# A fused attention and feed-forward kernel: other places for output steps, maxima and scales in a batch's first pair, none kept back in its last

## The chip, the cores and the metric

The kernel runs on one core of a Trainium2 chip. The metric is the device time of one execution in microseconds (us), the median of several runs; lower is better. The engines named here are TensorE (PE in the profile, its weight loads PEld), VectorE (DVE), ScalarE (ACT), GpSimd (POOL) and SyncE (SP), whose queue issues the DMAs.

## The reference

Sigmoid attention over 8 batches of 12 heads, 448 tokens and 64 columns, then a feed-forward layer with an ELU between two matrices (768 x 2048 and 2048 x 768). Everything is float32 at the borders.

```python
S = q.shape[2]
scores = np.matmul(q, k.transpose(0, 1, 3, 2)) / np.sqrt(q.shape[-1]) - np.log(S)
attn = 1.0 / (1.0 + np.exp(-scores))
x = np.matmul(attn, v)                     # (B, H, S, D), then to (B*S, H*D)
h = x @ w_in
g = np.where(h > 0.0, h, np.exp(np.minimum(h, 0.0)) - 1.0)
out = g @ w_out
```

## The kernel before

To keep float32 accuracy at the speed of float16 matmuls, nearly every operand is split into a high and a low float16 part (`split`: ScalarE writes the high part, VectorE the rest), and each product is made of three matmuls (high by high, and the two mixed ones). A split needs a scale, a power of two from the largest absolute value of the operand.

The twelve heads of a batch are worked on as six **pairs** (hp = 0 to 5). The batch loop over b = 1 to 7 does two things at once: the attention of batch b, and the second feed-forward matmul (`moe2`) of batch b-1, whose work is cut into **steps** of three matmuls of 128 x 384. Sixteen steps make one output tile; the sixteenth also issues the tile's eviction on VectorE (o, L537) and its output DMA. There are 96 steps where b is odd and 128 where it is even (`left`, L689). `fill(n)` puts n of them in. When the six pairs are through, the first feed-forward matmul of batch b (`moe1`, 288 matmuls on L499) follows.

TensorE, ScalarE, VectorE and SyncE take their instructions in the order in which the loop from L697 writes them (`tc.manual_schedule`, L685); each engine works through its own list in that order. GpSimd, and what is issued ahead of L685, is placed by the framework's scheduler. That concerns batch 1, whose first pairs still share the engines with the preparation of `w_out` (`load_w_out`, lines so, wo, L138 to L157, and splits on L121/L122).

For one pair n the order of the loop before is:

- `scores(0)`, `soften(0)`, `scores(1)`, `soften(1)`: six matmuls each into psc (two buffers of PSUM), then a sigmoid on ScalarE (sg, L395), the high part on ScalarE (at, L413) and the low part on VectorE (at, L414).
- `third()`: for pair n+1 the splits of q and k (nat) and of v (vn), and the DMA transpose of nat on SP. It needs the scales of pair n+1. The loads of pair n+3 follow on SP.
- `fill(gap)`, the first gap: 8 steps in a batch's first pair, 5 in the others.
- `prepare_pair(n+2)`, here called the **maxima**: VectorE's reductions of rv and raw for pair n+2 (mx and mt, L125, then L307 and L310) and three diagonal tiles (dg, L105). It returns `second`.
- `scores(2)`, `soften(2)`, `scores(3)`, `soften(3)`; number 3 has half the rows and needs no split. `scores(3)` needs the psc buffer that the second sigmoid reads.
- in the last pair the first part of `rescale` (rr L448, xh L450).
- `fill(share - gap - tail)`.
- `second()`, here called the **product**: one TensorE matmul of the diagonal tiles (pb, L110), VectorE's reduction and four to five tiny operations (al to L285), and GpSimd's scalar operations (L319, L322, L324, L289) that make the scales for the next `third`. It returns `third`.
- `values(0..3)`: 18 matmuls (L433) and two in float32 (L425) into pav; `finish`: the split of pav into xh (ACT L121, DVE L122) and a maximum over it.
- in the last pair four steps that were kept back (`tail`), then `moe1`, which starts with `xh` of pair 0 and reaches that of pair 5 with its sixteenth matmul; after its eighteenth stands one pb matmul for the scale of the whole of xh.

PSUM: psc 2 x 2 banks, pav one bank, and the tag pm with three banks, shared by the output tiles, pb and most of moe1.

Of the kernel before, what the change touches and what calls it, by code (L numbers as in the profile page):

```python
# [32 lines left out]
def attention_ffn(  # L33
# [13 lines left out]
    NP = H // 2  # L47
# [208 lines left out]
    def load_qk(b, hp):  # L256

        h0 = 2 * hp
        raw = sb.tile([P, 2 * NC + 1, 2, D], F32, tag="raw", name=f"raw{b}_{hp}", bufs=2)
        for i, src in enumerate((q, k)):  # L260
            for j in range(2):
                nc.sync.dma_start(  # L262
                    raw[:, i * (NC + 1) :][:, :NC, j],
                    src[b, h0 + j, :SM].rearrange("(p c) d -> p c d", c=NC),
                )
            nc.sync.dma_start(
                raw[rows[i], NC], src[b, h0 : h0 + 2, SM:].rearrange("h r d -> r h d")
            )
        return raw

    def load_v(b, hp):
        rv = rvs[(b * NP + hp) % len(rvs)]
        main = rv[:, : 2 * NC].rearrange("p t d -> p (t d)")
        load_keys(main, [rv[r, 2 * NC + j] for j, r in enumerate(rows)], v, b, 2 * hp)
        return rv
# [270 lines left out]
    def out_scale(b, xs, xp, i=slice(0, NH)):  # L546
        if b % 2 == 0 and i.start == 0:
            oscs[0] = sb.tile([P, 3, NH], F32, tag="osc", name=f"osc{b}", bufs=2)
        j = b % 2
        o = oscs[0][:, j, i]  # L550
        nc.gpsimd.tensor_scalar(
            o, wop[:, i], wm[:, 0:1], 2.0 ** (10 - XTOP + 2 - GTOP - WTOP),
            op0=ALU.mult, op1=ALU.mult,
        )
        nc.gpsimd.tensor_scalar(o, o, xs[:, 0, NP - 1 :], xp, op0=ALU.mult, op1=ALU.mult)
        nc.gpsimd.tensor_copy(oscs[0][rows[j], 2, i], o[rows[j]])

    def moe2(b, g, wo):
        j = b % 2
        osc = oscs[0]  # L560

        def tokens(b, c):
            if c < NC:
                return out[b * S : b * S + SM].rearrange("(p c) m -> c p m", c=NC)[c]
            return out[b * S + SM : (b + 1) * S]

        def tile_of(c, i):
            if c < NC:
                return moe2_tile(
                    wo, [(slice(0, P), tokens(b, c))],  # L570
                    lambda gj, f: g[:, gj, f, c * P : (c + 1) * P],
                    osc[:, j, i : i + 1], i, f"{b}_{c}_{i}",
                )
            return moe2_tile(
                wo, [(rows[a], tokens(b - 1 + a, NC)) for a in range(2)],
                lambda gj, f: g[:, gj, f, SM:],
                osc[:, 2, i : i + 1], i, f"{b}_r_{i}",
            )

        for i in range(NH):  # L580
            for c in range(NC + j):
                yield from tile_of(c, i)
# [3 lines left out]
    def step(n):  # L586
        for _ in range(n):
            next(steps, None)
# [7 lines left out]
    def prepare_pair(n):  # L596

        if n >= len(pairs):
            return lambda: lambda: None
        b, hp = pairs[n]  # L600
        if hp == 0:
            xh_of[b] = sb.tile([P, NK, 2, S], F16, tag="xh", name=f"xh{b}", bufs=2)
            xs_of[b] = sb.tile([P, 3, NP], F32, tag="xs", name=f"xs{b}", bufs=2)
        scales = prepare(b, hp, *loaded.pop(n), xs_of[b])

        def second():
            transposed = scales()

            def third():
                ready[n] = transposed()  # L610

            return third

        return second
# [12 lines left out]
    def pair_of(n):  # L627
        b, hp = pairs[n]
        return Pair(b, hp, *ready.pop(n), xh_of[b], xs_of[b])

    def hidden(b, beside=None):

        xh, xs = xh_of.pop(b), xs_of.pop(b)
        whole = rescale(b, xh, xs)
        next(whole)
        yield
        xp, xr, rest = next(whole)
        m = sb.tile([P, 2, NF], F32, tag="msc", name=f"msc{b}")

        def first():  # L640
            rest()
            moe_scales(m, xs, xr)

        moe1(b, g, xh, m, first, beside)
        yield b, xs, xp
# [29 lines left out]
    third = prepare_pair(EXACT * NP + 1)()  # L675
# [9 lines left out]
    with tc.manual_schedule(engines={E.PE, E.Activation, E.DVE, E.SP}):  # L685
        for b in range(EXACT, B):
            out_scale(*of_moe2, slice(0, 1 if b == EXACT else NH))
            tiles = moe2(b - 1, g, wo)
            left = NF * NH * (NC + (b - 1) % 2)  # L689

            def fill(n):
                nonlocal left
                left -= n
                for _ in range(n):
                    next(tiles, None)

            for hp in range(NP):  # L697
                n = b * NP + hp
                share = left // (NP - hp)
                tail = 4 if hp == NP - 1 else 0  # L700
                p = pair_of(n)
                for t in range(2):
                    p.scores(t)
                    p.soften(t)
                third()
                if n + 3 < len(pairs):
                    loaded[n + 3] = load_qk(*pairs[n + 3]), load_v(*pairs[n + 3])

                gap = 8 if hp == 0 else 5
                fill(gap)  # L710
                second = prepare_pair(n + 2)
                for t in range(2, NC + 1):
                    p.scores(t)
                    p.soften(t)
                if b == EXACT and hp < NC:

                    step(3 if hp < NC - 1 else NF)
                if hp == NP - 1:
                    h = hidden(b)
                    next(h)  # L720
                fill(share - gap - tail)
                third = second()
                for t in range(NC + 1):
                    p.values(t)
                p.finish()
                fill(tail)
                if b == EXACT and hp == NC - 1:
                    out_scale(*of_moe2, slice(1, NH))
            of_moe2 = next(h)
        out_scale(*of_moe2)  # L730
        for _ in moe2(B - 1, g, wo):
            pass
# [30 lines left out]
```

## Time and profile before

| | |
|---|---|
| median of 3 runs | 1271.4 us (1270.87 to 1273.9) |
| profiled execution, its own time | 1270.86 us |
| its span, first to last instruction | 1269.1 us |
| mean granted TensorE clock | 0.984 |
| VectorE busy | 823.4 us, 65% of the span |
| ScalarE busy | 671.8 us, 53% |
| TensorE on moe1 (L499) / moe2 (L529, po) | 442.0 / 392.9 us |

All times within the execution are counted from the first instruction. A row of the timeline reads: start, duration, engine, line, operation, output<-inputs, shapes, number of merged instructions, and in brackets the idle time of the engine before it with what ended it. Matmuls overlap in the pipeline, so a row's duration reaches a little into the next row's start; distances are read from start to start. A row of the waits reads: engine, what waited, what it waited for, us in total, times, the longest. A row of the windows gives, for a stretch, its length, the busy time of each engine with the number of instructions, the granted TensorE clock, and the DMA share with GB/s.

### The profile page before, as it was taken

To read this page: it belongs to the slowest core of one execution; us is meant where nothing else is said; L and a number is where in the kernel's file an instruction comes from. 1 tells how busy PE (TensorE), PEld (TensorE's weight loads), DVE (VectorE), ACT (ScalarE), POOL (GpSimd) and SP (SyncE) were. 2 spreads that over 40 slices of the span, in tenths; PEclk is the share of its full clock that TensorE was granted. 3 is DMA by queue.
4 is the path that set the end of the run, shared out by engine and by line. 5 is a ranking of instruction groups with operands and counts; after the bars stand their busy time and mean duration, and the time that the engine had idled before them with its cause. 6 is when DMAs were issued, how large, how long until landed. Compare 5 with 4: busy or idle time off the path is not lost.

```text
span 1269.1 us, 19337 instructions
## 1 busy us (share of the span) xinstructions
PE 1200.2 (95%) x7246; PEld 610.5 (48%) x7246; DVE 823.4 (65%) x1872; ACT 671.8 (53%) x1015; POOL 84.1 (7%) x319
## 2 busy tenths in 40 slices
PE   5979868999999999999999999999999999999998
PEld 2324334445555554545455554545455554455565
DVE  5898989765766557775666646885576656765500
ACT  5867777643655337744555436654565435663400
POOL 0011001100000000010000000010000100100000
PEclk9889979999999999999999999999999999999999
DMA  8937423420233103340144201440034401410000
GB/s 229 281 100 222 126 77 80 100 49 1 60 84 89 37 1 83 89 86 1 37 92 92 50 1 43 105 103 7 1 86 92 92 1 22 106 43 7 1 25 26
DMA packets 213407, 89.76 MB, mean 71 GB/s; under 512 B 177472, under 2 KB 209216, under 8 KB 213312
## 3 DMA queue, kind: packets, MB, share of 16 engines
q1 hardware_dynamic: 213312, 88.51, 28.7%
q8 instruction: 57, 0.93, 0.3%
q14 instruction: 38, 0.31, 0.1%
HBM read 58.20 MB, written 11.01 MB: 55 GB/s over the span
## 4 chain that ended last, share of the span: by engine, by line
PE 78%; ACT 8%; DVE 7%; DMA 3%; issue 2%; SPq 2%; DVEq 0%; POOL 0%; ACTq 0%; POOLq 0%
PE ph L499 31%; PE po L529 25%; PE psc L384 7%; PE pav L433 6%; PE po_r L529 5%; PE pav L425 3%; ACT sg L395 2%; DMA stage<-in_moe_w_in_dram 2%; ACT at L413 1%; SPq L262 1%; PE pb L110 1%; ACT L395 1%; ACT e L511 1%; DVE e L514 1%; DMA so<-in_moe_w_out_dram 1%
## 5 line engine op out<-in xcount | busy, mean ns | idle before, releaser
L499 PE MATMUL ph<-xh,wi 128*128 128x448 f16 x2304 | 442.0, 353 | 6.1 <-DVE xh L122 2.4
L529 PE MATMUL po<-wo,g 128*128 128x384 f16 x2304 | 392.9, 328 | 0.0
L529 PEld LDWEIGHTS <-g 128*128 128x128 f16 x2688 | 257.2, 98 | 198.4 <-issue 36.3
L499 PEld LDWEIGHTS <-wi 128*128 128x128 f16 x2304 | 225.3, 98 | 218.4 <-issue 7.6
L511 ACT ACTIVATE e<-ph,msc 128x448 f32<-128x448 f32 x128 | 80.8, 633 | 211.7 <-PE ph L499 211.6
L414 DVE SCALAR_TENSOR_TENSOR at<-sg,at 128x896 f16<-128x896 f32 x126 | 137.2, 1090 | 84.5 <-ACT at L413 84.5
L395 ACT ACTIVATE sg<-psc,bias,sc 128x896 f32<-128x896 f32 (+1 forms) x168 | 166.6, 992 | 1.7
L513 DVE TENSOR_SCALAR e<-e 128x448 f32<-128x448 f32 x128 | 50.3, 394 | 170.8 <-ACT e L511 170.7
L121 ACT ACTIVATE xh<-pav,sc 128x448 f16<-128x448 f32 x48 | 30.3, 632 | 216.7 <-PE pav L425 216.7
L384 PE MATMUL psc<-qk 64*128 64x448 f16 x1008 | 116.6, 355 | 11.4 <-ACT sg L395 11.4
L413 ACT ACTIVATE at<-sg 128x896 f16<-128x896 f32 x126 | 119.8, 951 | 4.1
L121 ACT ACTIVATE g<-e,msc 128x384 f16<-128x384 f32 (+1 forms) x192 | 96.0, 534 | 6.0 <-DVE e L514 4.3
L122 DVE SCALAR_TENSOR_TENSOR g<-e,msc,g 128x384 f16<-128x384 f32 (+1 forms) x192 | 94.6, 521 | 0.6
L514 DVE SCALAR_TENSOR_TENSOR e<-ph,msc,e 128x448 f32<-128x448 f32 x128 | 87.3, 683 | 4.0
L384 PEld LDWEIGHTS <-qk 64*128 64x128 f16 x1008 | 41.7, 97 | 89.7 <-issue 60.2
L433 PE MATMUL pav<-at,vn 128*64 128x448 f16 x756 | 80.2, 357 | 0.0
L324 POOL TENSOR_SCALAR sc<-pw 128x1 f32<-128x1 f32 x42 | 12.4, 295 | 843.5 <-DVE pw L114 790.9
L529 PE MATMUL po_r<-wo,g 128*128 128x384 f16 x384 | 64.7, 326 | 0.0
L122 DVE SCALAR_TENSOR_TENSOR xh<-pav,sc,xh 128x448 f16<-128x448 f32 x48 | 32.7, 680 | 48.7 <-ACT xh L121 48.7
L433 PEld LDWEIGHTS <-vn 128*64 128x64 f16 x756 | 39.4, 110 | 50.0 <-issue 27.8
L122 DVE SCALAR_TENSOR_TENSOR nat<-raw,sc,nat 128x384 f16<-128x384 f32 (+1 forms) x126 | 59.1, 524 | 0.0
L121 ACT ACTIVATE nat<-raw,sc 128x384 f16<-128x384 f32 (+1 forms) x126 | 58.8, 529 | 0.0
(103 smaller groups left out, 852.7 us busy)
## 6 DMA issues: line engine op xcount, KB each, us to landing
stage<-in_moe_w_in_dram SPq DMA_DIRECT2D x16, 768.0 KB, 6.6
raw<-in_q_dram SPq DMA_DIRECT2D x96, 96.0 KB, 3.1
raw<-in_k_dram SPq DMA_DIRECT2D x96, 96.0 KB, 2.6
rv<-in_v_dram SPq DMA_DIRECT2D x48, 192.0 KB, 2.7
out_dram<-o SPq DMA_DIRECT2D x48, 192.0 KB, 2.1
wo<-in_moe_w_out_dram SPq DMA_DIRECT2D x19, 384.0 KB, 4.1
so<-in_moe_w_out_dram SPq DMA_DIRECT2D x13, 384.0 KB, 4.3
raw<-in_q_dram SPq DMA_DIRECT2D x48, 32.0 KB, 2.4
```

Source lines behind the costliest of these rows:

```text
L121: nc.scalar.mul(hi, src, s)
L122: nc.vector.scalar_tensor_tensor(lo, src, s, hi, op0=ALU.mult, op1=ALU.subtract)
L384: nc.tensor.matmul(psc[:, j, :S] if g < NC else psc[rows[j], 0, :S], kk[rows[j], o], qq[rows[j], :S], start=(n == 0), stop=(n == len(parts ...
L395: a = nc.scalar.activation(sg[:, :nb], psc[:, :nb, :S], AF.Sigmoid, bias=bias, scale=self.s_scale)
L413: nc.scalar.mul(hi, sg, 2.0**ATOP)
L414: nc.vector.scalar_tensor_tensor(lo, sg, 2.0**ATOP, hi, op0=ALU.mult, op1=ALU.subtract)
L433: nc.tensor.matmul(pav[rows[j], :S], vv[i][:, j * NC + g], sg[k][:, j], start=(g == 0 and n == 0), stop=False,)
L499: nc.tensor.matmul(ph[:, :S], wi[:, wj, c, f * P : (f + 1) * P], xh[:, c, xj], start=(n == 0), stop=(n == 3 * NK - 1),)
L511: a = nc.scalar.activation(e, ph[:, :S], AF.Exp, scale=inv)
L513: nc.vector.tensor_scalar(e, e, 1.0, -1.0, op0=ALU.min, op1=ALU.add)
L514: nc.vector.scalar_tensor_tensor(e, ph[:, :S], inv, e, op0=ALU.mult, op1=ALU.max)
L529: nc.tensor.matmul(po[:, :HM], lh(gj, f), wo[:, i, f, wj], start=(n == 0), stop=(n == 3 * NF - 1),)
```

## The change

In a batch's first pair (hp = 0) the first gap has 11 steps, and the pair 3 more in all; the other pairs share what is left. There the maxima come behind `scores`/`soften` 2 and 3, so behind VectorE's third split, and the product isn't issued at the pair's end but in the second pair, behind its first two `scores`; `third` follows it there after `soften` 0 and 1 as before. In every pair the two `scores` are written ahead of both `soften`, which leaves each engine's own order as it was. In the last pair no steps are kept back: all stand ahead of the product.

```diff
             for hp in range(NP):
                 n = b * NP + hp
-                share = left // (NP - hp)
-                tail = 4 if hp == NP - 1 else 0
+                share = left // (NP - hp) + (3 if hp == 0 else 0)
                 p = pair_of(n)
                 for t in range(2):
                     p.scores(t)
+                if hp == 1:
+                    third = second()
+                for t in range(2):
                     p.soften(t)
                 third()
                 if n + 3 < len(pairs):
                     loaded[n + 3] = load_qk(*pairs[n + 3]), load_v(*pairs[n + 3])
 
-                gap = 8 if hp == 0 else 5
+                gap = 11 if hp == 0 else 5
                 fill(gap)
-                second = prepare_pair(n + 2)
+
+                if hp:
+                    second = prepare_pair(n + 2)
                 for t in range(2, NC + 1):
                     p.scores(t)
                     p.soften(t)
+                if not hp:
+                    second = prepare_pair(n + 2)
...
-                fill(share - gap - tail)
-                third = second()
+                fill(share - gap)
+                if hp:
+                    third = second()
                 for t in range(NC + 1):
                     p.values(t)
                 p.finish()
-                fill(tail)
```

The steps of the six pairs, worked out from the code: where b is odd 16 each before, and 19, 15, 15, 15, 16, 16 now; where b is even 21, 21, 21, 21, 22, 22 before (the last with 4 kept back), and 24, 20, 21, 21, 21, 21 now.

## The prediction

> **What bounds the kernel now.** I read the page's first part, then TensorE's own waits, then the timeline wherever one of those waits stands.
>
> ```profile
> PE 1200.2 (95%) x7246; PEld 610.5 (48%) x7246; DVE 823.4 (65%) x1872; ACT 671.8 (53%) x1015; POOL 84.1 (7%) x319
> ...
> PE psc L384 <- ACT sg L395: 14.4, 13, 2.5
> PE pb L110 <- DVE dg L105: 11.6, 6, 2.0
> ```
>
> TensorE is busy for 95% of the span, so only its idle time can be won, as long as the number of matmuls stays the same (it does). The two waits above are what the change aims at: `scores(3)` that waits for the second sigmoid to free its psc buffer, and the product's matmul that waits for the diagonal tiles of the maxima. The timeline shows where they are. This is the first pair of batch 3 (odd, 96 steps):
>
> ```profile
> 472.99 1.31 PE L384 MATMUL psc<-qk 64*128 64x448 f16 x12
> ...
> 474.24 4.07 PE L529 MATMUL po<-wo,g 128*128 128x384 f16 x24
> ...
> 478.24 0.74 PE L384 MATMUL psc<-qk 64*128 64x448 f16 x6
> ...
> 478.88 1.08 ACT L395 ACTIVATE sg<-psc,bias,sc 128x896 f32<-128x896 f32 x1
> ...
> 480.01 0.76 PE L384 MATMUL psc<-qk 64*64 64x448 f16 x6 [1.03 <-ACT sg L395]
> ...
> 483.77 0.95 ACT L413 ACTIVATE at<-sg 128x896 f16<-128x896 f32 x1
> 483.84 0.68 DVE L125 TENSOR_REDUCE mx<-rv 128x1 f32<-128x512 f32 x1
> ...
> 486.11 0.58 DVE L105 TENSOR_SCALAR dg<-eye,mx 128x128 bf16<-128x128 bf16 x3
> ...
> 486.75 0.32 PE L110 MATMUL pb<-dg,ones 128*128 128x384 bf16 x1 [1.97 <-DVE dg L105]
> ...
> 487.00 1.89 PE L433 MATMUL pav<-at,vn 128*64 128x448 f16 x18
> ...
> 488.13 0.55 DVE L112 TENSOR_REDUCE al<-pb 128x3 f32<-128x384 f32 x1
> ...
> 489.38 0.16 DVE L285 RECIPROCAL xs<-xs 128x1 f32<-128x1 f32 x1
> ...
> 489.77 1.31 PE L384 MATMUL psc<-qk 64*128 64x448 f16 x12
> ```
>
> The pair takes 489.77 - 472.99 = 16.78 us, of which TensorE waits 1.03 + 1.97 = 3.00. Eight steps go from 474.24 to 478.24: **0.50 us a step**. In an even batch (128 steps) the second wait is covered by more steps; only the first is left:
>
> ```profile
> 326.36 1.08 ACT L395 ACTIVATE sg<-psc,bias,sc 128x896 f32<-128x896 f32 x1
> ...
> 327.49 0.76 PE L384 MATMUL psc<-qk 64*64 64x448 f16 x6 [1.22 <-ACT sg L395]
> ```
>
> **Part 1: first gap, maxima and product in the first pair.** Three more steps delay `scores(2)` by 1.5 us. Batch 3: it starts at 479.74, `scores(3)` some 0.7 later at 480.4; the sigmoid ends at 478.88 + 1.08 = 479.96. Batch 2: `scores(3)` comes at 327.7, the sigmoid ends at 327.44. Both waits go.
>
> Nothing stands between the second fill and the values any more; what is late next is VectorE's third split. Its input is ready at 483.77 + 0.95 = 484.72 and VectorE was free at 483.84, so it ends 1.09 later, at 485.8. Without the waits and the product (0.25, from 486.75 to 487.00), but with three steps more, the pair takes 16.78 - 3.00 - 0.25 + 1.50 = 15.03 us. The values then start at 485.25 (2.77 ahead of the end) and need the third split after two thirds of their 1.8 us, at 486.5: 0.7 to spare.
>
> The maxima take 2.85 us (483.84 to 486.69), so they end at 485.8 + 2.85 = 488.65. The product now stands behind two `scores` of pair 1, at 488.02 + 1.25 = 489.27: no wait. First pair of an odd batch: **-1.75 us**, with three steps more done.
>
> The price is paid in pair 1. The chain behind the product (488.13 to 489.54, 1.41 us of VectorE) now stands ahead of its first split. Rows of pair 1:
>
> ```profile
> 489.90 0.40 POOL L322 COPY sc<-sc 64x1 f32<-64x1 f32 x2
> ...
> 492.67 1.09 DVE L414 SCALAR_TENSOR_TENSOR at<-sg,at 128x896 f16<-128x896 f32 x1 [0.92 <-ACT at L413]
> ...
> 494.51 1.40 ACT L121 ACTIVATE nat<-raw,sc 128x384 f16<-128x384 f32 x3
> 494.64 1.09 DVE L414 SCALAR_TENSOR_TENSOR at<-sg,at 128x896 f16<-128x896 f32 x1 [0.87 <-ACT at L413]
> ...
> 499.77 0.58 DVE L105 TENSOR_SCALAR dg<-eye,mx 128x128 bf16<-128x128 bf16 x3
> ...
> 500.40 0.32 PE L110 MATMUL pb<-dg,ones 128*128 128x384 bf16 x1
> ...
> 544.41 1.31 PE L384 MATMUL psc<-qk 64*128 64x448 f16 x12
> ```
>
> VectorE idles 0.92 + 0.87 = 1.79 us ahead of the two splits, both times for ScalarE. The chain's 1.41 us and some 0.4 us by which maxima and a tile's eviction run into the split of xh come to 1.8. So the first split is late by about 0.9, the second starts on time: cost 0, with **no margin**. The other end is the whole chain, 1.41 us a batch; I take 0, since the two idle rows are of this very place, and keep the rest for the range. ScalarE's split of nat waits for GpSimd's scales: they are ready 0.76 us after the chain's end (490.30 against 489.54), about 4.5 us into the pair, and ScalarE comes to nat at 494.51 - 489.77 = 4.74. `second` issues no DMA; `third` with its transpose, and the loads behind it on SP, keep their place.
>
> **Part 2: what three steps fewer bring to the other pairs.** Here I differ from a plain sum. Pairs 1 to 4 of batch 3 follow each other at (544.41 - 489.77) / 4 = 13.66 us. TensorE's own work makes 1.25 + 2.5 + 1.4 + 5.5 + 0.25 + 2.77 = 13.67 (scores, five steps, scores, eleven steps, product, values). But VectorE's diagonal tiles end at 499.77 + 0.58 = 500.35, and the product starts at 500.40: it starts as soon as it may. Both chains are as long. The one through sigmoids, splits and maxima (10.58 us into the pair) doesn't get shorter with a step less, so in odd batches pairs 1 to 3 stay at 13.66 and TensorE waits about 0.45 us more at pb (0.2 in pair 1, which has two products). The three steps bring nothing there. In even batches a pair has 20 to 22 steps, TensorE sets the pace, and the wait removed is won in full: **-1.22 us**.
>
> **Part 3: no steps kept back.** Last pair of batch 3:
>
> ```profile
> 555.05 0.32 PE L110 MATMUL pb<-dg,ones 128*128 128x384 bf16 x1 [1.91 <-DVE dg L105]
> ...
> 557.98 2.11 PE L529 MATMUL po<-wo,g 128*128 128x384 f16 x12
> ...
> 559.39 0.67 DVE L122 SCALAR_TENSOR_TENSOR xh<-pav,sc,xh 128x448 f16<-128x448 f32 x1
> ...
> 559.93 3.57 PE L499 MATMUL ph<-xh,wi 128*128 128x448 f16 x18
> ...
> 560.50 0.61 DVE L537 TENSOR_SCALAR o<-po,osc 128x384 f32<-128x384 f32 x1
> ...
> 561.21 0.25 DVE L105 TENSOR_SCALAR dg<-eye,rr 128x128 bf16<-128x128 bf16 x1
> ```
>
> The product waits 1.91; the four steps (557.98 to 559.93, 1.95) now fill that wait instead of standing behind the values. So moe1 starts about **1.85 us** earlier, at 558.1. It reads xh of pair 5 with matmul 16 (high) and 17 (low): at 0.19 us each that is 558.1 + 3.0 = 561.1. The low part ended at 560.06; the last eviction comes ahead of it now and adds 0.6: 560.65. 0.4 to spare. The diagonal for the scale of xh ends at 561.46, as before (the same operations in another order), and its matmul comes at 558.1 + 3.4 = 561.5: just in time. Batches 1, 3 and 5 win this. Even batches have no wait at that product, and batch 7 has no product there (no pairs follow): 0.
>
> **Part 4: batch 1 and the clock.**
>
> ```profile
> 198.43 1.17 PE L384 MATMUL psc<-qk 64*64 64x448 f16 x6 [1.23 <-ACT sg L395]
> ...
> 204.59 0.58 DVE L105 TENSOR_SCALAR dg<-eye,mx 128x128 bf16<-128x128 bf16 x3
> ...
> 206.12 0.33 PE L110 MATMUL pb<-dg,ones 128*128 128x384 bf16 x1
> ...
> 260.77 0.32 PE L110 MATMUL pb<-dg,ones 128*128 128x384 bf16 x1 [1.90 <-DVE dg L105]
> ```
>
> In batch 1 the first pair waits for the w_out work (loads, ScalarE), which the change doesn't shorten; three steps more fit into those waits. Then the second pair has a step less behind 198.43 (its product has 0.95 us of slack to the tiles): -0.5. The product out of the first pair: -0.25. The last pair as in batch 3: -1.85. Together **-2.6**; how the scheduler places w_out's instructions anew can make that 0 or -4.
>
> ```profile
> 781.02 0.32 PE L110 MATMUL pb<-dg,ones 128*128 128x384 bf16 x1 [1.97 <-DVE dg L105]
> ...
> 782.30:785.70 3.40, 3.40 (x14) 1.02 (x12) 1.38 (x7) 0.00 (x0) 1.12 (x5) 0.50 0.57 127
> ```
>
> In batch 5 the clock is granted at 0.50 for 3.4 us right behind the 1.97 us wait: 1.7 us of matmuls lost. With the wait gone I expect that stretch to go: **-1.7**. The Trainium skill ("TensorE: Matmul & The Clock Gate", section "HAM oscillation — how this bites in real kernels") says that TensorE must not idle for more than about 3.4 us at a time; by that rule a wait of 1.97 costs no clock, and the stretch would have another cause and stay. The row speaks against it: 1.97 us sufficed here. By the rule the sum would be 1.7 smaller.
>
> **The sum.** Batches 3 and 5: 2 x (1.75 + 1.85) = 7.2; batch 7: 1.75; batches 2, 4, 6: 3 x 1.22 = 3.7; batch 1: 2.6; clock: 1.7. Together 16.95 us off the profiled execution's 1270.86 (span 1269.1 and 1.8 around it): 1253.9. The median of the runs shown lies 0.5 above: **1254.5 us**, 1.3% faster.
>
> **Rivals.**
> (a) *The pairs run at TensorE's pace*: if the 10.6 us chain of VectorE shrinks with the steps, pairs 1 to 3 of the four odd batches win 3 x 0.5 - 0.25 = 1.25 each: 5 us more, 1249.5. Against it: pb starts 0.05 behind the tiles in the row at 500.40.
> (b) *The half-clock stretch stays*: with no tie between wait and clock, 1.7 us less is won: 1256.2. For it: the same wait at 486.75 has no such stretch behind it.
> (c) *Pair 1 is late and batch 1 wins nothing*: the chain's 1.41 us comes through in four odd batches (5.6; even ones have TensorE work to cover it), and 2.6 in batch 1 fall out: 1262.7. For it: no margin in Part 1.
> (d) *Nothing covers the start of moe1*: the four steps stood between the values and the split of xh. Batch 0 has no such steps:
>
> ```profile
> 89.14 3.20 PE L499 MATMUL ph<-xh,wi 128*128 128x448 f16 x16 [0.70 <-DVE xh L450]
> ...
> 94.78 3.52 PEld L499 LDWEIGHTS <-wi 128*128 128x128 f16 x20 [2.88 <-DVE xh L122]
> 94.78 3.96 PE L499 MATMUL ph<-xh,wi 128*128 128x448 f16 x20 [2.44 <-DVE xh L122]
> ```
>
> There moe1 waits 0.70 + 2.44 = 3.14 us. Seven times that is 22.0 and gives 1276.5: slower. It starts to count when the low part of xh ends later than 3.0 us after moe1's start, and turns the change into a loss from 16.95 / 7 = 2.4 us a batch. Against it: in batch 0 VectorE still splits w_in ahead of xh, later it doesn't.
> (e) *The waits only move* (a little of c and d together): within 0.3%.
>
> **Chances.** Forecast 0.45, (a) 0.10, (b) 0.15, (c) 0.18, (d) 0.07, (e) 0.05. The range from 1248 to 1265 leaves out (d), (e) and the far ends of (a) and (c). A measurement of this kernel can tell about 0.3% (3.8 us) from no change: faster 0.88, same 0.05, slower 0.07.
>
> **What would show it.** Right: no wait of psc for sg in the first pairs from batch 2 on; pb in second pairs behind twelve score matmuls without a wait; small new waits of 0.2 to 0.6 us at pb in pairs 1 to 3 of odd batches, whose distance stays near 13.7; moe1 directly behind the float32 values, without a wait at L122; no half clock in batch 5. Wrong: a wait of 1 us or more at pb at the end of pair 1 (c), at xh L122 or at the pb inside moe1 (d), or odd pairs at 13.2 (a). More than one new half-clock stretch of 3.4 us would spoil the sum by 1.7 each.

## The result and the profile after

| | before | after |
|---|---|---|
| median | 1272.62 us (1270.87 to 1273.9, 4 runs) | 1257.97 us (1257.05 to 1258.93, 4 runs) |
| span of the profiled execution | 1269.1 | 1255.3 |

The ratio is 0.9886 with a 95% interval of 0.9868 to 0.9904: faster by 1.1%, 14.7 us between the medians. The prediction was 1254.5 with 1248 to 1265. Between the two profiled executions its sum was 16.95 us; the spans differ by 13.8, so the sum was 3.1 too large.

TensorE's waits after, from the view of the waits (us in total, times, longest), begin with:

```profile
PE psc L384 <- ACT sg L395: 11.8, 7, 3.7
PE so L150 <- DVE wo L143: 9.2, 4, 6.0
PE pb L110 <- DVE dg L105: 6.8, 11, 1.1
```

The waits for the diagonal tiles (pb) fell from 11.6 us in 6 to 6.8 us in 11: the long ones went, and small new ones came. Where the time went is read from the windows between one moe1 and the next, first before, then after, for batches 1, 2, 3, 5 and 7 (window, length, busy time of PE, PEld, DVE, ACT and POOL, clock, DMA):

```profile
162.18:265.65 103.47, 87.35 (x556) 42.88 (x555) 85.58 (x193) 72.42 (x106) 12.17 (x40) 0.92 0.39 92
320.35:418.36 98.01, 96.79 (x654) 50.48 (x655) 68.71 (x157) 57.40 (x78) 8.46 (x35) 1.00 0.37 83
473.06:559.93 86.87, 81.96 (x560) 41.10 (x559) 66.75 (x152) 57.03 (x76) 8.07 (x34) 1.00 0.42 90
...
767.34:855.80 88.46, 83.56 (x558) 41.45 (x559) 66.74 (x152) 57.03 (x76) 8.10 (x34) 0.98 0.41 90
...
1063.21:1147.58 84.37, 81.37 (x557) 40.90 (x557) 58.19 (x122) 55.22 (x72) 5.86 (x24) 1.00 0.29 65
```

```profile
161.28:263.78 102.50, 87.94 (x555) 42.99 (x554) 85.64 (x187) 72.62 (x107) 12.46 (x37) 0.92 0.37 90
318.74:415.47 96.73, 96.73 (x655) 50.37 (x656) 68.44 (x155) 56.72 (x77) 10.08 (x34) 1.00 0.37 83
470.17:553.96 83.79, 81.81 (x559) 40.98 (x560) 64.96 (x144) 56.58 (x75) 9.47 (x31) 1.00 0.43 90
...
760.34:844.13 83.79, 81.81 (x558) 40.98 (x559) 64.97 (x144) 56.57 (x75) 9.46 (x31) 1.00 0.41 91
...
1050.51:1133.77 83.26, 81.28 (x557) 40.78 (x557) 57.76 (x121) 54.78 (x71) 7.87 (x24) 1.00 0.30 68
```

| batch | us won, predicted | us won, measured |
|---|---|---|
| 1 | 2.6 | 0.97 |
| 2, 4, 6 (each) | 1.22 | 1.28 |
| 3 | 3.6 | 3.08 |
| 5 | 3.6 + 1.7 (clock) | 4.67 |
| 7 | 1.75 | 1.11 |

In even batches TensorE is now busy for the whole window (96.73 of 96.73). In batches 3, 5 and 7 it still idles for 2.0 us. Beside these windows, moe1 of batches 1, 3 and 5 takes 0.25 us longer each (in batch 3 from 553.96 to 608.91, 54.95; before from 559.93 to 614.63, 54.70), all of it ahead of the pb matmul for the scale of xh, and the stretch ahead of batch 1, which the change doesn't touch, ended 0.9 earlier (161.28 against 162.18).

What the prediction missed stands in the second pair. Its timeline in batch 3, after:

```profile
482.17 1.89 PE L433 MATMUL pav<-at,vn 128*64 128x448 f16 x18
...
484.95 1.31 PE L384 MATMUL psc<-qk 64*128 64x448 f16 x12
...
486.19 0.34 PE L110 MATMUL pb<-dg,ones 128*128 128x384 bf16 x1
...
488.51 0.16 DVE L285 RECIPROCAL xs<-xs 128x1 f32<-128x1 f32 x1
488.59 2.31 DVE L414 SCALAR_TENSOR_TENSOR at<-sg,at 128x896 f16<-128x896 f32 x2
488.74 1.01 POOL L319 TENSOR_SCALAR sc<-sc 128x3 f32<-128x3 f32 x1
...
489.81 1.67 POOL L322 COPY sc<-sc 64x1 f32<-64x1 f32 x2
...
491.51 0.91 ACT L121 ACTIVATE nat<-raw,sc 128x128 f16<-128x128 f32 x2 [1.11 <-POOL sc L322]
...
491.94 1.12 DVE L122 SCALAR_TENSOR_TENSOR nat<-raw,sc,nat 128x128 f16<-128x128 f32 x2 [0.51 <-ACT nat L121]
...
495.79 0.58 DVE L105 TENSOR_SCALAR dg<-eye,mx 128x128 bf16<-128x128 bf16 x3
...
496.42 0.32 PE L110 MATMUL pb<-dg,ones 128*128 128x384 bf16 x1 [1.12 <-DVE dg L105]
...
499.44 1.31 PE L384 MATMUL psc<-qk 64*128 64x448 f16 x12
```

The first pair went as forecast: no wait of the scores, none of the values, and pb behind twelve score matmuls without a wait. VectorE's chain ends at 488.67, and the second of its two splits begins in time. But GpSimd, which makes the scales from that chain, now works while VectorE splits, and its operations are drawn out: L319 takes 1.01 us, the two copies 1.67 together. In the timeline of before they took 0.23 and 0.40. ScalarE waits 1.11 us for the copies in the middle of nat, VectorE 0.51 for ScalarE, and the diagonal tiles begin 10.84 us into the pair (484.95 to 495.79) instead of 10.00 (489.77 to 499.77 before). TensorE waits 1.12 us for them, where 0.2 was forecast, and the pair takes 14.49 us (to 499.44) instead of 13.66.

### The profile page after: what moved, and what is told of

Read it like the earlier page. It is cut to its first block, busy times and chain, and to the rows that moved or that the text cites. A ratio compares the mean times of both kernels' runs of the same rounds, so it can differ in the third digit from the quotient of the medians.

```text
span 1255.3 us, 19337 instructions
## 1 busy us (share of the span) xinstructions
PE 1195.3 (95%) x7246; PEld 608.5 (48%) x7246; DVE 824.8 (66%) x1872; ACT 672.3 (54%) x1015; POOL 95.5 (8%) x319
## 4 chain that ended last, share of the span: by engine, by line
PE 68%; DVE 11%; ACT 11%; issue 4%; DMA 3%; SPq 2%; POOL 1%; DVEq 0%; ACTq 0%; POOLq 0%
PE ph L499 30%; PE po L529 19%; PE psc L384 6%; PE pav L433 5%; PE po_r L529 5%; ACT sg L395 4%; PE pav L425 3%; DMA stage<-in_moe_w_in_dram 2%; ACT at L413 2%; DVE mt L125 1%; DVE mx L125 1%; DVE dg L105 1%; DVE nat L122 1%; SPq L262 1%; ACT nat L121 1%
## 5 line engine op out<-in xcount | busy, mean ns | idle before, releaser
L414 DVE SCALAR_TENSOR_TENSOR at<-sg,at 128x896 f16<-128x896 f32 x126 | 137.1, 1089 | 81.2 <-ACT at L413 80.7
```

The costliest lines, as they stand in the source:

```text
L414: nc.vector.scalar_tensor_tensor(lo, sg, 2.0**ATOP, hi, op0=ALU.mult, op1=ALU.subtract)
```

## The experiments

The theory (A) by then: every part is worth what the prediction's steps say, and the missing time in odd batches is GpSimd's, held up by VectorE's splits. The rival (B): VectorE alone is too full in the second pair. The first four kernels take the change apart and try A against B.

**The last pair's steps alone.**

```diff
-                tail = 4 if hp == NP - 1 else 0
+                tail = 0
```

> The kernel before with the steps kept back in the last pair removed, and nothing else. By the prediction's Part 3, the product's wait of 1.9 us in the last pair of batches 1, 3 and 5 is filled and moe1 starts some 1.85 us earlier there; even batches and batch 7 give 0; moe1 of odd batches may lose 0.1 to 0.3 at its scale's matmul. In all 4.5 to 5.5 us off: about 1265.5 to 1266.5 in an execution like the profiled one of before (1270.86). By the rival that nothing covers moe1's start, a wait for xh L122 of up to 3 us appears in seven batches and the time doesn't fall, or rises.

Measured: ratio 0.9966 (0.9953 to 0.998), median 1268.01 against 1272.43, profiled span 1265.9. The wait at the product in the last pairs is gone and moe1 waits for no xh from batch 1 on. The timeline of batch 3's last pair:

```profile
554.56 0.58 DVE L105 TENSOR_SCALAR dg<-eye,mx 128x128 bf16<-128x128 bf16 x3
555.19 0.32 PE L110 MATMUL pb<-dg,ones 128*128 128x384 bf16 x1
...
558.12 3.57 PE L499 MATMUL ph<-xh,wi 128*128 128x448 f16 x18
...
561.48 0.25 DVE L105 TENSOR_SCALAR dg<-eye,rr 128x128 bf16<-128x128 bf16 x1
561.79 0.22 PE L110 MATMUL pb<-dg,ones 128*128 128x128 bf16 x1
```

The matmul for the scale of xh starts 0.06 behind its diagonal (561.73), as close as the prediction had it. Rival (d) is out. The profiled execution took 1267.66 us, its span 3.2 less than that of before, where 4.5 to 5.5 was expected. From batch 2 on it holds two stretches at half clock (last section) where before has one, which costs 1.7 us; without that it is 4.9. The medians differ by 4.4.

**The first gap alone.**

```diff
-                share = left // (NP - hp)
+                share = left // (NP - hp) + (3 if hp == 0 else 0)
...
-                gap = 8 if hp == 0 else 5
+                gap = 11 if hp == 0 else 5
```

> The kernel before with 11 steps in the first gap and three more in the first pair, maxima and product at their old places, steps kept back as before. Theory (VectorE's chain of maxima sets the end of an odd first pair): the wait at the third and fourth scores goes in all batches, but in batches 3, 5 and 7 the first pair still ends when the diagonal tiles do, the wait at the product only shrinks from 1.97 to about 1.4, and pairs 1 to 3 don't get shorter with a step less, so odd batches win nothing; even ones win 1.22 each. In all 3.7 to 4.5 us off: about 1266.5 to 1267. Rival, the plain sum of idle time: 1.03 in each odd batch as well, 7 us or more off, about 1263.

Measured: ratio 0.9959 (0.9946 to 0.9972), median 1267.52. Even batches win 1.13 us each (96.88 against 98.01); batch 3 takes 86.84, batch 7 84.36, as before (86.87, 84.37). Its first pairs of batch 3:

```profile
485.60 0.32 PE L110 MATMUL pb<-dg,ones 128*128 128x384 bf16 x1 [1.60 <-DVE dg L105]
...
499.25 0.32 PE L110 MATMUL pb<-dg,ones 128*128 128x384 bf16 x1 [0.44 <-DVE dg L105]
```

The wait of 1.03 us is gone, but with three steps more and 1.60 us at pb the product starts 13.75 us into the first pair (471.85 to 485.60), as before (13.76). The later pairs wait 0.44 each and still follow at 13.65. The plain sum of idle time would have promised 3 us more.

**The product back at the first pair's end.** The call of `second` for hp = 0 goes back ahead of the values; the maxima stay behind the third split.

```diff
-                if hp == 1:
-                    third = second()
...
-                if hp:
-                    third = second()
+                third = second()
```

> The changed kernel with the product put back to the end of the first pair, ahead of its values (maxima stay behind the third split). Theory: the product then waits for the maxima, 485.7 against 482.2 in batch 3, so a wait of some 3.5 us in odd first pairs and of some 1.3 in even ones; pair 1 gets back to 13.66 us without a second product, which returns 0.7 to 0.9. In all 10 to 13 us slower than the changed kernel's 1257: about 1267 to 1270, so the two moves belong together. Rival: it is the maxima's place alone that pays, and the product's place is worth under 2 us: 1258 to 1259.

Measured: ratio 1.0016 (1.0005 to 1.0028), median 1275.21: a little slower than the kernel before, 17 us above the changed one. In batch 3:

```profile
489.35 0.48 PE L110 MATMUL pb<-dg,ones 128*128 128x384 bf16 x1 [3.53 <-DVE dg L105]
489.76 3.57 PE L433 MATMUL pav<-at,vn 128*64 128x448 f16 x18
```

The wait is the one worked out, 3.53 us in odd batches and 1.28 in even ones. The loss is larger than expected: batch 1 waits as well (3.47), and at two of the waits the clock is halved for 6.8 and 3.4 us (here 3.57 us for 18 matmuls instead of 1.89). As 1.5 us of that lie within a wait, this costs some 4.4 in the profiled execution. So the maxima's new place pays only together with the product's.

**The rest rows split last.** In `third` the splits of nat go q, k, then v, and the rest rows, whose scale comes out of the copies, last.

```diff
-                (0, NC, sc[:, 1:2]), (NC, 1, s_rest), (NC + 1, NC, sc[:, 2:3])
+                (0, NC, sc[:, 1:2]), (NC + 1, NC, sc[:, 2:3]), (NC, 1, s_rest)
             ):
+                if n_t == 1:
+                    split(vn[:, 0], vn[:, 1], rv[:, : 2 * NC], sc[:, 0:1])
...
-            split(vn[:, 0], vn[:, 1], rv[:, : 2 * NC], sc[:, 0:1])
```

> The changed kernel with the splits of third in another order: q, k, v and only then the rest rows, whose scale comes out of GpSimd's copies last. The same instructions, one moved. Theory A (GpSimd's scale operations are held up while VectorE runs its splits, 1.0 us instead of 0.23 and 1.67 for two copies instead of 0.40, and ScalarE waits 1.1 us for them): ScalarE's wait at nat in pair 1 goes, the wait at the product at the end of pair 1 in batches 3, 5 and 7 falls from 1.12 to 0.4 to 0.6, 1.5 to 2.1 us off: about 1255. Theory B (VectorE alone is too full in pair 1, as the prediction feared with the 1.41 us chain, and GpSimd plays no part): the wait at the product stays at 1.1 and the time at 1257.

Measured: ratio 0.9884 (0.9868 to 0.9901), median 1258.37; the time can't be told from that of the changed kernel, so the 1.5 to 2.1 us expected don't show in the medians. The trace differs (line numbers are up to three higher here):

```profile
485.13 1.31 PE L385 MATMUL psc<-qk 64*128 64x448 f16 x12
...
488.58 1.07 DVE L415 SCALAR_TENSOR_TENSOR at<-sg,at 128x896 f16<-128x896 f32 x1
488.73 1.01 POOL L319 TENSOR_SCALAR sc<-sc 128x3 f32<-128x3 f32 x1
...
495.76 0.32 PE L110 MATMUL pb<-dg,ones 128*128 128x384 bf16 x1 [0.27 <-DVE dg L105]
...
498.79 1.31 PE L385 MATMUL psc<-qk 64*128 64x448 f16 x12
```

GpSimd is as slow as in the changed kernel (1.01 us, ending 0.09 behind VectorE's split), but ScalarE no longer waits for it, and the wait at pb falls from 1.12 to 0.27. Theory B expected 1.1. The pair is back at 13.66 us (485.13 to 498.79), the length that the prediction gave it. The odd windows fall by 0.4 to 0.6 only (batch 3: 83.18); a part goes to the second pair's scores, which wait 0.14 to 0.22 for qk, since v now stands ahead of the rest rows and the transpose.

**The changed kernel again, and GpSimd's operations on VectorE.**

> The changed kernel once more, unaltered, so that the versions beside it are compared on the same chip. 1257 to 1259; in the trace the wait at the product at the end of pair 1 of batches 3, 5 and 7 is 1.1 us again and ScalarE waits 1.1 us for GpSimd's copies at nat, since the order of the instructions sets both.

Measured: median 1258.18, ratio 0.9888 (0.9867 to 0.9909); 1.12 at pb and 1.1 at nat again.

```diff
-                nc.gpsimd.tensor_scalar(sc[:, :n], sc[:, :n], 2.0**TOP, None, op0=ALU.mult)
+                nc.vector.tensor_scalar(sc[:, :n], sc[:, :n], 2.0**TOP, None, op0=ALU.mult)
...
-                    nc.gpsimd.tensor_copy(sc[r, n + 1 : n + 2], sc[r, 1 + i : 2 + i])
+                    nc.vector.tensor_copy(sc[r, n + 1 : n + 2], sc[r, 1 + i : 2 + i])
```

> The changed kernel with three of GpSimd's scale operations (the factor on the three scales and the two copies) put on VectorE, for every pair from batch 1 on. Theory A (GpSimd is held up by VectorE's splits): ScalarE's wait at nat for L322 goes; VectorE's chain in pair 1 gets about 0.55 us longer and its second split starts that much later, so the wait at the product at the end of pair 1 falls only from 1.12 to about 0.8 to 1.0; other pairs keep their distance of 13.66, since the operations lie ahead of a wait of VectorE for xh there. 0.5 to 1.5 us off: 1256 to 1257. Theory B (VectorE alone is too full): the chain's 0.55 us come on top, the wait grows to 1.6 to 1.7, and the time to about 1259.

Measured: median 1259.13, ratio 0.9893 (0.9876 to 0.9911): no faster. The wait at pb goes the way of theory A: ScalarE's wait is gone and pb waits 0.77, with more work on VectorE, where B had 1.6. The time doesn't fall, for another reason. The end of batch 3's second pair, then its last pair:

```profile
496.48 0.32 PE L110 MATMUL pb<-dg,ones 128*128 128x384 bf16 x1 [0.77 <-DVE dg L105]
...
557.62 0.54 PE L499 MATMUL ph<-xh,wi 128*128 128x448 f16 x2 [0.20 <-DVE xh L122]
...
558.63 0.22 PE L110 MATMUL pb<-dg,ones 128*128 128x128 bf16 x1 [0.47 <-DVE dg L105]
```

The same half microsecond on VectorE stands ahead of the split of xh there, and the 0.4 us to spare of the prediction's Part 3 is used up: moe1 takes 0.7 us longer (55.68) in batches 1, 3 and 5.

**The product a pair on in all pairs but the last**, and the maxima behind the third split there too; with the splits' order of rest_last, and with q, k, rest, v:

```diff
-                if hp == 1:
+                if hp:
                     third = second()
...
-                if hp:
+                if hp == NP - 1:
                     second = prepare_pair(n + 2)
...
-                if not hp:
+                if hp < NP - 1:
                     second = prepare_pair(n + 2)
...
-                if hp:
+                if hp == NP - 1:
                     third = second()
```

> The splits' order of rest_last, and in pairs 1 to 4 as well the maxima behind the third split and the product a pair on (pair 5 keeps both at the old places, for the next batch). Theory: with the product out of the way the values of odd batches no longer wait for the diagonal tiles, so the waits of 0.43 at pb go and pairs 1 to 4 run at TensorE's pace, 13.2 to 13.4 us with 15 steps and 13.7 with 16; attention of batches 3 and 5 takes about 82.2 to 82.8 us instead of 83.8; even batches stay at 96.7. In all 3 to 5 us below the changed kernel: 1252 to 1254. Rival (VectorE is full: some 12.6 us of work in each odd pair, and GpSimd held up in each): new waits at the scores for sg or qk, and no gain: 1257 or more.

> As defer_all, but with the splits in the order q, k, rest, v: the transpose of nat leaves 0.6 us earlier, and ScalarE may wait up to 0.6 us for GpSimd's copies. Theory: the waits of the first scores of a pair for qk (0.14 to 0.2 us in rest_last) go; within 1 us of defer_all either way. If GpSimd's delay is what counts, defer_all is the faster by 0.5 to 2 us; if the DMA's is, this one.

Measured: 1248.59 (ratio 0.981, 0.9793 to 0.9828) and **1247.53** (0.9806, 0.9784 to 0.9828). Both beat the changed kernel by some 10 us, more than expected. The second order is ahead in span (1245.2 against 1246.7): by some 0.7 ahead of batch 2, and by 0.25 in each later odd batch, about the scores' wait for qk that it takes away (0.2). The times of the runs overlap (up to 1248.94). Batch 3 with q, k, rest, v:

```profile
467.72:548.91 81.19, 81.19 (x559) 40.96 (x559) 65.37 (x144) 56.60 (x75) 17.64 (x31) 1.00 0.42 93
```

TensorE is busy for the whole window. GpSimd's 17.64 us for 31 operations, against 8.07 for 34 before, show that it is held up in pair after pair now. With the product behind the next pair's first scores, TensorE has no wait left that this could lengthen.

**Without the three steps more.**

```diff
-                share = left // (NP - hp) + (3 if hp == 0 else 0)
+                share = left // (NP - hp)
```

> The changed kernel with the first gap at 11 steps but without the three more in the first pair (16 or 21 steps there, the others as before the change). By Part 2 the three steps bring nothing to the odd batches' later pairs, so taking them out of the first pair should shorten it, up to the next limit: the values then reach the third split about 1.0 us too early and wait for it, so a first pair of 14.0 instead of 14.85 us at the most, and the second pair's chain starts at the same absolute time, which takes most of it back. Attention of batches 3 and 5: 83.3 to 83.8 us against 83.8, with waits at pb near 0 in pairs 2 and 3; even batches 96.7 as now. In all 0 to 2 us below the changed kernel: 1256 to 1258. Rival (the steps were worth their 1.5 us in the later pairs): odd batches 84.5 to 85.3 us, 1260 to 1263.

Measured: median 1258.55, ratio 0.9877 (0.9854 to 0.9901): the changed kernel's time. Batch 3 takes 83.60 (83.79 with the steps), even batches 96.73 in both. Of the first pair in batch 3:

```profile
487.24 0.38 PE L433 MATMUL pav<-at,vn 128*64 128x448 f16 x2 [0.56 <-DVE at L414]
...
488.95 1.31 PE L384 MATMUL psc<-qk 64*128 64x448 f16 x12 [0.39 <-DMA qk<-nat]
```

The values wait for the third split and the scores for qk; the waits at pb in pairs 2 and 3 are gone. Three steps in or out of the first pair change nothing here. That the gap of 11 is what brings the even batches' gain follows from the wait that it removes; no kernel has the other parts with a gap of 8.

## Why the prediction was right, and where it was off

- **Part 1, first pair.** Right: 482.17 for the values' start is 12.07 us into the pair (forecast 12.26), and the next pair starts 14.85 us in (forecast 15.03). Even batches 1.28 for 1.22.
- **Part 1, the price in pair 1.** This is the step that failed in size: "cost 0, with no margin" was 0.83 us (14.49 for 13.66), 2.5 in batches 3, 5 and 7 together. With the 1.6 by which batch 1 fell short and the 0.75 of moe1 (both below) that is 4.9 us, more than the 3.1 by which the sum was off. The rest is luck: the stretch ahead of batch 1 ended 0.9 earlier, and first, last and even pairs each won a little more than forecast. VectorE's part held (its second split starts at the forecast time); what was wrong is the sentence that GpSimd's scales "are ready 0.76 us after the chain's end". They took 2.8 (488.67 to 491.48). The 0.76 was read from a stretch in which VectorE idled (from 489.54 to 490.55 in before), and used for one in which it runs splits. rest_last and scales_dve show it from two sides. In the whole trace of the changed kernel the seven L319 that begin during a split at L414, whose two large inputs (sg, at) lie in SBUF, take 0.98 to 1.06 us and end 0.09 behind it. The four that begin during a split of xh, one of whose inputs (pav) lies in PSUM, take 0.23, as do the 29 beside an idle VectorE. The Trainium skill ("SBUF — State Buffer", section "Who interferes with whom") says that GpSimd shares a pair of SBUF ports with VectorE, that the pair is an exclusive lock, and that a VectorE instruction with two inputs in SBUF contends for it with a GpSimd instruction that reads SBUF. The rows agree: in rest_last L319 begins 0.15 behind the start of a split and ends 0.09 behind its end.
- **Part 2.** Right: pairs 2 and 3 wait 0.43 to 0.44 at pb (forecast 0.45) and stay at 13.65 (pair 1 is the point above); gap_only and no_plus3 show that steps given to or taken from them don't count in odd batches. Rival (a) is out for this change. defer_all shows where it would be right: once the product is off the path, TensorE's pace does set the time.
- **Part 3.** Right: 13.56 us from the last pair's start to moe1 in batch 3 (540.40 to 553.96) against 15.52 before. moe1's own 0.25 us, forecast as "just in time", is the one loss.
- **Part 4, batch 1.** Mis-sized: 0.97 for 2.6. Its last pair won its 1.9 and the first 0.5, but the second pair lost some 1.6: its scores wait 3.13 us for sg instead of 2.51, and the half clock behind lasts twice as long, 6.8 us instead of 3.4:

```profile
196.80:203.60 6.80, 5.67 (x20) 2.51 (x20) 6.01 (x14) 5.60 (x9) 3.34 (x6) 0.50 0.04 14
```

  Batch 1's window came out between 100.15 and 102.94 us in the kernels that carry the change or go beyond it, so its term can't be read from one trace. How much of this is the placement of w_out's instructions and how much the clock was not tried apart.
- **Part 4, the clock.** The stretch in batch 5 went, as forecast, and batch 5 now takes what batch 3 takes (83.79 each, where 88.46 and 86.87 stood). Rival (b) had for it that the same wait at 486.75 had no such stretch behind it; the last section shows what set the two apart.

## What to carry to other kernels

Idle time on the bounding engine is worth its sum only where no second chain is as long; the start-to-start distance of equal stages, beside the work in one stage and the time at which the other chain lets go, tells which it is. When an operation is moved, take its duration from rows in which the same neighbours run: tiny GpSimd operations beside VectorE's two-input splits took four times what they took beside an idle VectorE (1.01 for 0.23 us, 1.67 for 0.40). A result that is needed only in the next stage can be asked for there; here that was worth some 10 us in the other pairs, about as much as the change without its last-pair part (14.7 less the 4.4 of tail_only).

## What the runs showed of the hardware that was not expected

The granted clock can fall on a wait of 2 us. From batch 2 on (and in batch 1's last pair), the traces of the kernel before, tail_only, gap_only and product_end hold 15 waits of 1.9 us or more at pb; a stretch at half clock of 3.4 or 6.8 us begins at 5 of them, each time within or right behind the wait. Two of them, from tail_only:

```profile
485.50:488.90 3.40, 3.40 (x19) 1.45 (x18) 2.40 (x8) 0.00 (x0) 0.87 (x5) 0.50 0.54 122
1072.60:1076.00 3.40, 3.40 (x19) 1.56 (x16) 2.12 (x8) 0.00 (x0) 1.12 (x5) 0.50 0.55 124
```

In the seven traces whose waits there are 1.2 us at most (the changed kernel twice, rest_last, scales_dve, both deferred ones, no_plus3) there is none behind batch 1's second pair, until the program's last microseconds.

Which 5 of the 15 it is, the traces show too. The stretches of one trace begin whole multiples of 3.413 us apart: in before 198.63 and 782.31 (171 times), in tail_only 485.49 and 1072.58 (172), in product_end 487.85 and 1081.77 (174). Cut each trace into windows on that grid: from batch 2 on, TensorE idles for 1.96 to 2.85 us in the window ahead of each of the five stretches, and for 1.90 or less in every other window, until the last microseconds. Two waits of 1.97 us in before, the one at 781.02 and the one at 486.75, lie like this (length, then PE busy):

```profile
778.90:782.31 3.41, 1.44 (x14) 0.66 (x14) 3.28 (x9) 0.72 (x2) 0.00 (x0) 1.00 0.88 174
485.35:488.76 3.41, 2.02 (x19) 0.93 (x18) 3.24 (x11) 0.00 (x0) 0.00 (x0) 1.00 0.79 160
```

The first lies whole in its window, which has 1.97 us of idle time, and half clock follows. Of the second 1.39 us lie in the window, the rest in the one ahead of it, and none follows. So a wait of 1.97 us cost 1.7 us more where it fell whole into one such window. Where the grid lies differs from execution to execution (its first border is 0.66 us from the start in before, 0.80 in tail_only, 3.16 in product_end), so a part of the spread between runs may come from that; this wasn't tried. In the batches before, the border between the two isn't as sharp. Against it stands the rule that the prediction takes from the Trainium skill ("TensorE: Matmul & The Clock Gate", section "HAM oscillation — how this bites in real kernels"), by which such a wait costs no clock; here the measurement decides.
